# A narrower fifth turn in attention, with the last 64 keys' low parts made on VectorE

## The chip, the cores and the metric

The kernel runs on one core of one Trainium2 chip. The metric is the device time of one execution in microseconds (us); lower is better. TensorE (PE in the profile) multiplies matrices and writes to PSUM; its weight loads are shown as an engine of their own, PEld. VectorE is DVE, ScalarE is ACT, GpSimd is POOL, and SyncE (SP) issues the transfers.

## The reference

Three stages follow each other: attention with a threshold on four batches of 576 tokens and 8 heads of 64, a feed-forward layer with squared ReLU, and a mixture of eight experts of which each token takes one. The change is in the first stage alone. Cut to its core, that stage is:

```
scores = scale * np.matmul(q, k.transpose(0, 1, 3, 2))          # (4, 8, 576, 576)
thresh = np.max(scores, axis=-1, keepdims=True) - tau
scores = np.where(scores >= thresh, scores, -1000000000.0)
scores = scores - np.max(scores, axis=-1, keepdims=True)
attn = np.exp(scores)
attn = attn / (np.sum(attn, axis=-1, keepdims=True) + 1e-09)
attn_out = np.matmul(attn, v)
x = attn_out.transpose(0, 2, 1, 3).reshape(4 * 576, 512)
x = _moe_ref(x, w_in, w_out)      # np.maximum(x @ w_in, 0) ** 2 @ w_out
return _moe2_ref(x, w_gate, w_output_gate, w1, w2)              # top expert of eight
```

## The kernel before

**Precision.** Values that must be exact enough to choose an expert are split into a high part (rounded to the format float32r) and a low part (what is left), and a product is made of hi·hi, hi·lo and lo·hi.

**Pairs and chunks.** Attention runs over 16 pairs of heads (4 batches of 4 pairs; `pr` is the pair's number, `NP` is 4). A pair has 9 chunks of 128 query rows. A chunk goes through these steps, each on one engine:

1. scores (PE, L647): 128 x 576 into one of two PSUM buffers;
2. the row maximum (DVE, L650), the exponential (ACT, L653), the threshold (ACT, L658), mask and row sum (DVE, L662);
3. the reciprocal of the sum (POOL L667, DVE L670) and the normalisation of the 576 columns of the buffer `p` (POOL L673, or ACT L705);
4. outside the first batch, two small steps on POOL, `tail1` and `tail2` (L499 on 64 columns, and L718): they put the low parts of the last 64 keys into columns 576 to 639 of `p`, beside their plain values in columns 512 to 575;
5. the turn (PE, L727): five transposes of 128 x 128, one for each 128 columns of `p`, into one PSUM buffer of five blocks, `pT`. There is one `pT` buffer. The fifth block holds the last 64 keys in its rows 0 to 63, and in rows 64 to 127 their low parts (zeros in the first batch);
6. the evacuation of `pT`: in the first batch one copy on ACT (L738). Later ACT rounds all five blocks to the high part (`hi`, L744), and then DVE subtracts it from the first four blocks (`lo`, L747) to get the low part. When `lo` is done, `pT` is free for the next turn.

Then `t_av` multiplies the turned probabilities with the values: in plain float32 for the first batch (L788), in high and low parts after it (L770).

**What else runs in the stage.** The preparation of the next pair transposes k and q on PE (L570) and splits them on ACT (L578, L580) and DVE (L586, L588); its PSUM buffers are the two `pM` buffers, which `t_av` and the feed-forward matmuls (L866) use too. From the second batch on, feed-forward matmuls of finished batches are laid between the chunks. In the second batch DVE, ACT and POOL also convert the weights `w_in`.

**The order.** No order is written by hand. Every step is handed to a planner, `g.add(engine, duration, function, reads, writes, key)`. The planner lays the steps out with those assumed durations, takes the earliest that can start and among these the one with the smallest key, and hands out the buffers. The instructions then run on each engine in that order and wait for each other by semaphores. So a changed duration or a removed step moves others on all engines.

Of the kernel before, what the change touches and what calls it, by code (L numbers as in the profile page):

```python
# [257 lines left out]
def moa(ctx, tc, q, k, v, tau, w_in, w_out, wg, wog, w1, w2, ctab, coln, out):  # L258
    nc = tc.nc
    B, H, S, D = 4, 8, 576, 64  # L260
    P = 128
# [233 lines left out]
    for x in ALL["p"].slots:  # L495
        nc.gpsimd.memset(x.view[:, S:], 0.0)

    def gcopy(out, in_):
        nc.gpsimd.tensor_scalar(out, in_, 1.0, 1.0, op0=ALU.mult, op1=ALU.mult)  # L499

# [125 lines left out]
    def t_chunk(n, key):  # L626
# [79 lines left out]
                  key + K("norm", pr))  # L706
        else:
            g.add("POOL", 0.73, nrm, [sm], [p], key + K("norm", pr))
        if not full(pr, 0):
            ph = new("pk", n)  # L710
            last, low = slice(512, S), slice(S, NQ * P)

            def tail1():
                gcopy(ph.t, p.t[:, last])

            def tail2():

                nc.gpsimd.tensor_tensor(p.t[:, low], p.t[:, last], ph.t.bitcast(F32), op=ALU.subtract)  # L718

            g.add("POOL", 0.16, tail1, [p], [ph], key + K("norm", pr))  # L720
            g.add("POOL", 0.27, tail2, [ph], [p], key + K("norm", pr))
# [2 lines left out]

        def tr():
            for j in range(NQ):
                nc.tensor.transpose(ps.t[:, j], p.t[:, j * P : (j + 1) * P], ident)  # L727

        g.add("PE", 0.545, tr, [p], [ps], key + K("turn", pr))
        for j, gi, c0, w, off in PARTS[st]:  # L730
            h = 2 * pr + j
            whole = full(pr, j)
            if (h, gi) not in ptb:
                ptb[h, gi] = new("ptf" if whole else "pt", f"{h}_{gi}")
            pt = ptb[h, gi]
            if whole:
                g.add("ACT", c_act(NQ * w, True),
                      lambda pt=pt, c0=c0, w=w, off=off: nc.scalar.activation(  # L738
                          pt.t[:, :, off : off + w], ps.t[:, :, c0 : c0 + w], AF.Copy),
                      [ps], [(pt, 0, off)], key + K("parts", pr))  # L740
                continue

            def hi(pt=pt, c0=c0, w=w, off=off):
                nc.scalar.activation(pt.t[:, :NQ, off : off + w], ps.t[:, :, c0 : c0 + w], AF.Copy)  # L744

            def lo(pt=pt, c0=c0, w=w, off=off):
                nc.vector.tensor_tensor(  # L747
                    pt.t[:, NQ:, off : off + w], ps.t[:, : NQ - 1, c0 : c0 + w],
                    pt.t[:, : NQ - 1, off : off + w].bitcast(F32), op=ALU.subtract,
                )  # L750

            g.add("ACT", c_act(NQ * w, True), hi, [ps], [(pt, 0, off)], key + K("parts", pr))
            g.add("DVE", c_dve(4 * w), lo, [ps, (pt, 0, off)], [(pt, 1, off)], key + K("parts", pr))

    def t_av(pr, j, gi, key):
        h = 2 * pr + j
        pt = ptb.pop((h, gi))
        N = GN[gi]
        vb = vh.get(pr)
        ps = Buf(pM, f"av{h}_{gi}")  # L760
        if pr not in xfb:
            xfb[pr] = new("xf", pr)
        xf = xfb[pr]
        mine = slice(64 * j, 64 * j + 64)
        other = slice(64 - 64 * j, 128 - 64 * j)
        cols = slice(GOFF[gi], GOFF[gi] + N)

        def mm(lo):
            for c in range(NQ - 1, 2 * NQ - 1) if lo else range(NQ - 1):
                nc.tensor.matmul(  # L770
                    ps.t[:, :N], vb.t[:, j, c % NQ].rearrange("p a d -> p (a d)"), pt.t[:, c, :N],
                    start=(c == 0), stop=(c == 2 * NQ - 2),
                )

        def e1():
            nc.scalar.activation(xf.t[mine, cols], ps.t[other, :N], AF.Copy)

        def e2():
            nc.vector.tensor_tensor(xf.t[mine, cols], ps.t[mine, :N], xf.t[mine, cols], op=ALU.add)

        offs = [0, 128] if gi == 0 else [0, 128, 256]
        if full(pr, j):
            raw = raws[pr, "v"]

            def mm1():
                for c in range(NQ):
                    kr = QSZ[c]
                    nc.tensor.matmul(ps.t[:64, :N], raw.t[:kr, j, c], pt.t[:kr, c, :N],  # L788
                                     start=(c == 0), stop=(c == NQ - 1))

            g.add("PE", NQ * 4 * N * 0.4227e-3 + 0.06, mm1, [(pt, 0, o) for o in offs] + [(raw, j), (raw, 2)], [ps], key, hold=[xf])
            g.add("ACT", c_act(N, True), lambda: nc.scalar.activation(xf.t[mine, cols], ps.t[:64, :N], AF.Copy),
                  [ps], [(xf, j, gi)], key)
            return
        for hl in range(2):
            rd = [(pt, x, o) for o in offs for x in range(1 + hl)] + [(vb, j, x) for x in range(2)]
            g.add("PE", (NQ - 1 + hl) * c_pe(N), lambda hl=hl: mm(hl), rd, [ps], key, hold=[xf])
        g.add("ACT", c_act(N, True), e1, [ps], [(xf, j, gi)], key)
        g.add("DVE", c_dve(N), e2, [ps], [(xf, j, gi)], key)
# [629 lines left out]
```

## Time and profile before

| | |
|---|---|
| median of 3 runs | 1042.99 us (1042.43 to 1044.68) |
| profiled execution | 1044.39 us, of which the span of its instructions is 1042.6 us |
| granted TensorE clock over the span | 0.993 of full speed |
| PE busy | 95% of the span |
| PEld busy | 84% |
| DVE, ACT, POOL busy | 66%, 62%, 33% |

By the timestamps of the turn the four batches of attention take about 16 to 484 us: the first until about 124 us, the second until about 240 us, the third and fourth until about 484 us. Each batch has 36 chunks. A busy PE is not the same as a PE at its peak: matmuls overlap, and the record of one matmul (270 to 400 ns) is longer than the distance to the next one. The distance from start to start tells what a matmul costs in a row of them.

### The profile page before, as it was taken

What the parts mean: (1) busy time and instruction counts of PE and PEld (TensorE: products, weight loads), DVE (VectorE), ACT (ScalarE), POOL (GpSimd) and SP (SyncE); (2) the same over time, 40 slices, a digit from 0 to 9 for tenths busy, and PEclk for the clock granted to TensorE, in tenths of its full rate; (3) what the DMA queues carried; (4) which work ended last, traced back from release to release, by engine and by line L of the source; (5) the groups of instructions that cost most, each with busy time, mean ns of one, the idle gap of its engine ahead of it and who ended that gap; (6) DMA issues with size and microseconds to landing.
All of it is one profiled execution on the core that took longest, in us unless ns stands there. A gap on an engine that the chain in (4) does not pass through costs nothing.

```text
span 1042.6 us, 19065 instructions
## 1 busy us (share of the span) xinstructions
PE 995.4 (95%) x6276; PEld 876.4 (84%) x6276; DVE 693.0 (66%) x1563; ACT 645.3 (62%) x1347; POOL 345.2 (33%) x660
## 2 busy tenths in 40 slices
PE   6999888999999999999999999999999999999995
PEld 5666588889999999999998888888789988888884
DVE  4768989987877777885652444434587768767730
ACT  5778776676766666766643444444665668767730
POOL 1233788675665666562000000010112211211200
PEclk9999989999999999999999999999999999999998
DMA  6555766554455554544882344433757868877700
GB/s 150 123 135 143 174 169 173 159 135 126 119 124 142 141 136 122 154 121 130 248 254 60 104 120 118 118 108 82 222 166 262 289 204 283 292 256 256 277 21 24
DMA packets 165438, 167.86 MB, mean 161 GB/s; under 512 B 60367, under 2 KB 126159, under 8 KB 165330
## 3 DMA queue, kind: packets, MB, share of 16 engines
q1 hardware_dynamic: 161090, 156.03, 52.3%
q0 software_dynamic: 4096, 10.52, 3.1%
q8 instruction: 52, 0.85, 0.4%
q14 instruction: 56, 0.46, 0.2%
q10 hardware_dynamic: 144, 0.00, 0.0%
HBM read 110.72 MB, written 29.56 MB: 135 GB/s over the span
## 4 chain that ended last, share of the span: by engine, by line
PE 72%; DMA 8%; DVE 8%; issue 5%; ACT 4%; POOL 1%; SPq 0%; DVEq 0%; POOLq 0%; ACTq 0%
PE bank L981 17%; PE bank L866 14%; PE bank L1295 9%; PE bank L1245 8%; PE bank L727 6%; PE bank L647 6%; PE bank L770 5%; PE bank L788 3%; DMA memf<-in_moe_w_dram 2%; DMA memf<-in_moe_w_out_dram 2%; DVE memf L650 1%; DMA out_dram<-memf 1%; PE bank L1100 1%; PE bank L1265 1%; DVE memf L662 1%
## 5 line engine op out<-in xcount | busy, mean ns | idle before, releaser
L866 PE MATMUL bank<-memr,w 128*128 128x288 f32 x1536 | 228.9, 299 | 4.5 <-ACT memf L872 2.5
L866 PEld LDWEIGHTS bank<-memr,w 128*128 128x128 f32 x1536 | 209.8, 188 | 9.1 <-ACT memf L872 4.8
L981 PE MATMUL bank<-w,memr 128*128 128x512 f32 x648 | 157.4, 394 | 0.0
L981 PEld LDWEIGHTS bank<-w,memr 128*128 128x128 f32 x648 | 119.1, 188 | 23.4
L662 DVE SCALAR_TENSOR_TENSOR memf<-bank,memf 128x576 f32<-128x576 f32 x144 | 115.7, 813 | 34.5 <-ACT memf L653 33.6
L647 PE MATMUL bank<-memr 128*128 128x288 f32 x600 | 112.0, 315 | 7.1 <-DVE memf L662 6.7
L727 PE MATMUL bank<-ident,memf 128*128 128x128 f32 x720 | 106.4, 279 | 10.7 <-ACT ptf L738 5.0
L650 DVE TENSOR_REDUCE memf<-bank 128x1 f32<-128x576 f32 x144 | 106.2, 748 | 12.3 <-PE bank L647 9.5
L1086 POOL DMA_INDIRECT lst<-memf x18 | 18.1, 1008 | 267.5 <-DVE memf L1072 202.8
L673 POOL TENSOR_SCALAR memf<-memf 128x576 f32<-128x576 f32 x128 | 97.4, 765 | 26.4 <-DVE memf L670 14.5
L653 ACT ACTIVATE memf<-bank,memf 128x576 f32<-128x576 f32 x144 | 104.1, 734 | 0.2
L727 PEld LDWEIGHTS bank<-ident,memf 128*128 128x128 f32 x720 | 82.8, 142 | 23.3 <-issue 7.0
L647 PEld LDWEIGHTS bank<-memr 128*128 128x128 f32 x600 | 87.1, 194 | 12.1 <-DVE memf L662 10.0
L744 ACT ACTIVATE memr<-bank 128x640 fp32r<-128x640 f32 (+1 forms) x120 | 76.7, 650 | 22.8 <-PE bank L727 21.0
L1245 PE MATMUL bank<-memr,w 128*128 128x256 f32 x564 | 89.0, 283 | 0.6 <-DVE memr L1255 0.5
L966 DVE TENSOR_TENSOR memr<-memf,memr 128x512 fp32r<-128x512 f32 x72 | 48.3, 699 | 59.3 <-ACT memf L963 59.2
L1230 DVE TENSOR_TENSOR w<-memf,w 128x512 fp32r<-128x512 f32 x114 | 74.5, 687 | 13.6 <-ACT w L1227 10.8
L667 POOL TENSOR_SCALAR memf<-memf 128x1 f32<-128x1 f32 x144 | 31.3, 217 | 149.0 <-DVE memf L662 131.7
L747 DVE TENSOR_TENSOR memr<-bank,memr 128x512 fp32r<-128x512 f32 (+1 forms) x120 | 74.4, 628 | 8.3 <-ACT memr L744 7.2
L1245 PEld LDWEIGHTS bank<-memr,w 128*128 128x128 f32 x564 | 77.4, 191 | 1.8 <-DVE memr L1255 1.0
L1295 PE MATMUL bank<-memr 128*128 128x512 f32 x306 | 77.3, 393 | 0.0
L1230 DVE TENSOR_TENSOR memr<-memf,memr 128x512 fp32r<-128x512 f32 x94 | 62.7, 688 | 21.3 <-ACT memr L1227 14.8
(144 smaller groups left out, 1725.9 us busy)
## 6 DMA issues: line engine op xcount, KB each, us to landing
memf<-in_moe_w_dram SPq DMA_DIRECT2D x104, 512.0 KB
r_scr<-memf SPq DMA_DIRECT2D x128, 144.0 KB
memf<-r_scr SPq DMA_DIRECT2D x36, 512.0 KB
memr<-memr SPq DMA_DIRECT2D x64, 144.0 KB
memr<-memr SPq DMA_DIRECT2D x64, 128.0 KB
memr<-memr SPq DMA_DIRECT2D x32, 256.0 KB
memf<-in_moe_w_in_dram SPq DMA_DIRECT2D x16, 512.0 KB
memf<-in_moe_w_out_dram SPq DMA_DIRECT2D x16, 512.0 KB
```

The lines of the kernel that those rows point to most:

```text
L647: nc.tensor.matmul(s.t[:, hf, :HALF], qo, ko[:, halves[hf]], start=(i == 0), stop=(i == len(ops) - 1))
L650: nc.vector.tensor_reduce(nm.t, s.t[:, :, :HALF], axis=AX.XY, op=ALU.max, negate=True)
L653: nc.scalar.activation(p.t[:, :S].rearrange("p (a n) -> p a n", a=2), s.t[:, :, :HALF], AF.Exp, bias=nm.t)
L662: nc.vector.scalar_tensor_tensor(p3, s.t[:, :, :HALF], th.t, p3, op0=ALU.is_ge, op1=ALU.mult, accum_out=sm.t)
L673: nc.gpsimd.tensor_scalar(p.t[:, :S], p.t[:, :S], sm.t, 1.0, op0=ALU.mult, op1=ALU.mult)
L727: nc.tensor.transpose(ps.t[:, j], p.t[:, j * P : (j + 1) * P], ident)
L744: nc.scalar.activation(pt.t[:, :NQ, off : off + w], ps.t[:, :, c0 : c0 + w], AF.Copy)
L866: nc.tensor.matmul(ps.t[:, :HALF], wv[:, a, kc], xT.t[:, x, kc, half], start=(i == 0), stop=(i == len(seq) - 1),)
L981: nc.tensor.matmul(ps.t, s.t[:, fc], wob[fc].t[:, x], start=(fc == 0 and i == 0), stop=(fc == NFC - 1 and i == 2))
L1230: lambda i=i, w=w, raw=raw: nc.vector.tensor_tensor(w.t[:, 1], raw.t[:, i], w.t[:, 0].bitcast(F32), op=ALU.subtract),
L1245: nc.tensor.matmul(ps.t[:, :256], w1b[kc][fc // 4].t[:, a, (fc % 4) * P : (fc % 4 + 1) * P], x2.t[:, x, kc], start=(i == 0), stop=(i == 11))
L1295: nc.tensor.matmul(ps.t, hT.t[:, a, fc, u * P : (u + 1) * P], w2b[fc].t[:, x], start=(fc == 0 and i == 0), stop=(fc == 7 and i == 2))
```

## The change

The fifth turn transposes only the 64 columns of the last keys, so that it writes 64 rows of the fifth block, in every chunk of the first, third and fourth batch (108 of the 144 chunks). In the second batch (`early_low`) all stays as it was. For the third and fourth batch `tail1` and `tail2` on POOL are gone. In their place a new DVE step after `lo` subtracts the high part from rows 0 to 63 of the fifth block and writes the difference to rows 64 to 127 of the evacuated tile. Each chunk has one such step of 128 columns, the fifth of a pair's chunks has two of 64. The low-part matmuls of `t_av` wait for this step too. The planner's duration for a turn falls from 0.545 to 0.49 in the changed batches. One memset at the start clears the rows of `pT` that the narrow turn no longer writes.

```
+    nc.vector.memset(pT.slots[0].view()[64:, NQ - 1], 0.0)
...
-        if not full(pr, 0):
+        early_low = NP <= pr < 2 * NP
+        if early_low:
             ph = new("pk", n)
...
         def tr():
             for j in range(NQ):
-                nc.tensor.transpose(ps.t[:, j], p.t[:, j * P : (j + 1) * P], ident)
-
-        g.add("PE", 0.545, tr, [p], [ps], key + K("turn", pr))
+                m = P if j < NQ - 1 or early_low else 64
+                nc.tensor.transpose(ps.t[:m, j], p.t[:, j * P : j * P + m], ident)
+
+        g.add("PE", 0.545 if early_low else 0.49, tr, [p], [ps], key + K("turn", pr))
...
             g.add("DVE", c_dve(4 * w), lo, [ps, (pt, 0, off)], [(pt, 1, off)], key + K("parts", pr))
+            if not early_low:
+                g.add("DVE", 0.08 + w / 600,
+                      lambda pt=pt, c0=c0, w=w, off=off: nc.vector.tensor_tensor(
+                          pt.t[64:, NQ - 1, off : off + w], ps.t[:64, NQ - 1, c0 : c0 + w],
+                          pt.t[:64, NQ - 1, off : off + w].bitcast(F32), op=ALU.subtract),
+                      [ps, (pt, 0, off)], [(pt, 2, off)], key + K("parts", pr))
...
-            rd = [(pt, x, o) for o in offs for x in range(1 + hl)] + [(vb, j, x) for x in range(2)]
+            rd = [(pt, x, o) for o in offs for x in ((0, 1, 2) if hl else (0,))] + [(vb, j, x) for x in range(2)]
```

Two places show how the order moves. The first is on DVE, in the third batch, where a pair's q is prepared. `bank_2_73` is `pT`, `bank_1_68` and `bank_1_69` are the `pM` buffers, `bank_2_77` and `bank_2_78` are the score buffers. Before:

```order
L586 TENSOR_TENSOR memr<-bank_1_68,memr 128x384
L747 TENSOR_TENSOR memr<-bank_2_73,memr 128x4x128
L586 TENSOR_TENSOR memr<-bank_1_69,memr 128x192
L650 TENSOR_REDUCE memf<-bank_2_77 128x1
L588 SCALAR_TENSOR_TENSOR memr<-bank_1_68,qsc,memr 128x320
L650 TENSOR_REDUCE memf<-bank_2_78 128x1
L747 TENSOR_TENSOR memr<-bank_2_73,memr 128x4x128
L588 SCALAR_TENSOR_TENSOR memr<-bank_1_69,qsc,memr 128x256
```

And now, where the lines after the inserted code are up to 12 numbers higher (L747 is L753, the new step is L762):

```order
L589 TENSOR_TENSOR memr<-bank_1_69,memr 128x384
L673 RECIPROCAL memf<-memf 128x1
L753 TENSOR_TENSOR memr<-bank_2_73,memr 128x4x128
L762 TENSOR_TENSOR memr<-bank_2_73,memr 64x128
L589 TENSOR_TENSOR memr<-bank_1_68,memr 128x192
L591 SCALAR_TENSOR_TENSOR memr<-bank_1_69,qsc,memr 128x320
L653 TENSOR_REDUCE memf<-bank_2_77 128x1
L653 TENSOR_REDUCE memf<-bank_2_78 128x1
L591 SCALAR_TENSOR_TENSOR memr<-bank_1_68,qsc,memr 128x256
L753 TENSOR_TENSOR memr<-bank_2_73,memr 128x4x128
```

The new step stands right behind `lo`, and the first split of q (128x320) stands ahead of both row maxima, where it had one of them ahead of it.

The second place is on PE, in the third batch, towards the end of a pair's chunks. Before:

```order
L727 MATMUL bank_2_73<-ident,memf 128x128 x5
L866 MATMUL bank_1_69<-memr,w_84 128x288 x8
L647 MATMUL bank_2_78<-memr 128x288 x4
L866 MATMUL bank_1_68<-memr,w_84 128x288 x4
L727 MATMUL bank_2_73<-ident,memf 128x128 x5
L866 MATMUL bank_1_68<-memr,w_84 128x288 x8
L770 MATMUL bank_1_69<-memr 128x320 x9
L570 MATMUL bank_1_68<-ident,memf 128x128 x3
```

And now:

```order
L733 MATMUL bank_2_73<-ident,memf 128x128 x4
L733 MATMUL bank_2_73<-ident,memf 64x128
L878 MATMUL bank_1_68<-memr,w_88 128x288 x4
L650 MATMUL bank_2_77<-memr 128x288 x4
L878 MATMUL bank_1_69<-memr,w_88 128x288 x8
L733 MATMUL bank_2_73<-ident,memf 128x128 x4
L733 MATMUL bank_2_73<-ident,memf 64x128
L878 MATMUL bank_1_69<-memr,w_88 128x288 x4
L782 MATMUL bank_1_68<-memr 128x320 x9
L573 MATMUL bank_1_69<-ident,memf 128x128 x3
```

A turn still has five matmuls; the fifth writes 64 rows of 128 columns instead of 128 rows. Between two turns there still lie 12 feed-forward matmuls and four of a score, and in the last stretch of the pair four feed-forward matmuls where there were eight.

## Rows read from the trace of the kernel before

**Rows 1.** The page, busy time and share of each engine.

```profile
PE 995.4 (95%) x6276; PEld 876.4 (84%) x6276; DVE 693.0 (66%) x1563; ACT 645.3 (62%) x1347; POOL 345.2 (33%) x660
```

**Rows 2.** Busy time by stretch: first batch, second batch, third and fourth.

```profile
core 0: us, PE busy (x) PEld busy (x) DVE busy (x) ACT busy (x) POOL busy (x), PEclk, DMA share, GB/s
16.00:124.00 108.00, 98.28 (x543) 66.92 (x543) 79.82 (x186) 84.80 (x177) 39.89 (x76) 1.00 0.58 141
124.00:240.00 116.00, 105.98 (x755) 97.93 (x754) 103.07 (x222) 81.57 (x174) 91.29 (x169) 0.97 0.61 158
240.00:485.00 245.00, 243.56 (x1872) 237.88 (x1871) 194.08 (x443) 165.39 (x361) 144.58 (x336) 1.00 0.50 132
```

**Rows 3.** Waits of PE and PEld, 259 to 437 us: total, times, longest us.

```profile
PEld bank L866 <- DVE memr L588: 2.7, 6, 0.5
...
PE bank L866 <- DVE memr L588: 1.3, 6, 0.2
```

**Rows 4.** Lines by shape, 259 to 437 us: count, busy us, mean ns, idle before.

```profile
L727 PE MATMUL bank<-ident,memf 128*128 128x128 f32 x274 | 39.0, 273 | 0.0
...
L747 DVE TENSOR_TENSOR memr<-bank,memr 128x512 fp32r<-128x512 f32 x48 | 32.8, 682 | 1.8 <-ACT memr L744 1.6
...
L727 PEld LDWEIGHTS bank<-ident,memf 128*128 128x128 f32 x275 | 31.5, 140 | 0.8
...
L718 POOL TENSOR_TENSOR memf<-memf,memr 128x64 f32<-128x64 f32 x54 | 17.3, 324 | 3.5
...
L499 POOL TENSOR_SCALAR memr<-memf 128x64 fp32r<-128x64 f32 x54 | 13.0, 245 | 3.4
...
L747 DVE TENSOR_TENSOR memr<-bank,memr 128x256 fp32r<-128x256 f32 x12 | 4.5, 420 | 0.4
```

**Rows 5.** Timeline of turns and plain float32 matmuls: start us, length us, count.

```profile
330.77 0.71 PE L727 MATMUL bank<-ident,memf 128*128 128x128 f32 x5
...
330.72 0.20 PEld L727 LDWEIGHTS bank<-ident,memf 128*128 128x128 f32 x2
...
61.17 1.78 PE L788 MATMUL bank<-ptf,memf 128*64 128x320 f32 x6
```

**Rows 6.** Lines by shape, whole span: the plain float32 matmul.

```profile
L788 PE MATMUL bank<-ptf,memf 128*64 128x320 f32 x64 | 18.9, 439 | 0.0
```

**Rows 7.** Timeline of weight loads with fewer than 128 columns, and of those behind them.

```profile
60.58 0.19 PEld L788 LDWEIGHTS bank<-ptf,memf 128*64 128x64 f32 x2 [0.16 <-issue]
...
63.56 0.31 PEld L727 LDWEIGHTS bank<-ident,memf 128*128 128x128 f32 x3 [0.49 <-issue]
...
597.28 1.05 PEld L1015 LDWEIGHTS bank<-memr 128*32 128x32 f32 x8
...
598.34 0.31 PEld L981 LDWEIGHTS bank<-w,memr 128*128 128x128 f32 x2
```

**Rows 8.** Timeline of `lo` on DVE and of the turn's loads, third batch.

```profile
329.92 0.69 DVE L747 TENSOR_TENSOR memr<-bank,memr 128x512 fp32r<-128x512 f32 x1
...
333.07 0.69 DVE L747 TENSOR_TENSOR memr<-bank,memr 128x512 fp32r<-128x512 f32 x1
...
330.72 0.53 PEld L727 LDWEIGHTS bank<-ident,memf 128*128 128x128 f32 x5
...
333.87 0.53 PEld L727 LDWEIGHTS bank<-ident,memf 128*128 128x128 f32 x5
...
326.46 0.76 DVE L747 TENSOR_TENSOR memr<-bank,memr 128x256 fp32r<-128x256 f32 x2
```

**Rows 9.** Timeline around the split of q, third batch.

```profile
342.35 0.75 DVE L650 TENSOR_REDUCE memf<-bank 128x1 f32<-128x576 f32 x1
343.01 0.54 DVE L588 SCALAR_TENSOR_TENSOR memr<-bank,qsc,memr 128x320 fp32r<-128x320 f32 x1
...
342.14 0.53 ACT L580 ACTIVATE memr<-bank,qsc 128x320 fp32r<-128x320 f32 x1
...
343.60 3.28 PEld L866 LDWEIGHTS bank<-memr,w 128*128 128x128 f32 x24 [0.45 <-DVE memr L588]
```

## The prediction

> **What bounds the kernel now.** I read the busy time of the page first. PE is busy for 95% of the span [rows 1]; the reader is to see that no other engine comes near it. A mean over the whole span says little about a change to attention, so the stretches come next [rows 2]. They differ. In the third and fourth batch PE is busy for 243.56 of 245 us. In the first batch it is busy for 98.28 of 108 us, and in the second, which the change leaves alone but for the order, for 105.98 of 116 us, with DVE at 103.07. So in the third and fourth batch only two things can count: what shortens PE's own work, and what makes PE wait. The waits come third: in the 178 us from 259 to 437, six pairs of heads, PE and its weight loads have one wait worth naming, the feed-forward matmuls that wait for DVE to split q, 2.7 us for six pairs [rows 3]. No wait on POOL is among them. Last come the timelines, from which the spacing of matmuls and the distance from one step to the next are read [rows 5 to 9].
>
> **The narrow turn itself.** Five turns take 0.71 us from the first start to the last end, and one record is 0.273 us long [rows 4, 5]. So they follow each other by (0.71 - 0.273) / 4 = 0.109 us. Either the weight load sets this or the moving operand does. The load: two loads with records of 0.140 us take 0.20 us together, so the second starts 0.06 us after the first [rows 4, 5]; a load of 128 columns holds the next one up for 0.06 us, not for 0.109. The moving side: six plain float32 matmuls of 320 columns take 1.78 us with records of 0.439 us [rows 5, 6], which is (1.78 - 0.439) / 5 = 0.268 us each, or 0.84 ns a column; 128 columns at that rate are 0.107 us. That fits. In a transpose the 64 or 128 columns of `p` are the loaded operand and the 128 columns of the identity move; the order shows a fifth turn of 64 x 128, so the identity still moves all its 128 columns. I take a saving of nothing. The bounds: half a turn for each of 108 chunks, 108 x 0.055 = 5.9 us less, if the load did set the pace; and a loss, if a load of 64 columns empties the array first (the last rival).
>
> A rule of the Trainium skill stands against this reading: "TensorE: Matmul & The Clock Gate", section on LDWEIGHTS, has a load cost its columns divided by 1.2 GHz, 107 ns for 128 columns and 53 ns for 64. By that rule the turn would be bound by its load and the narrow one would give back 54 ns, an estimate of 5.8 us in all. The 0.06 us between two loads of turns disagrees with it, so I carry it as a rival only.
>
> **The two POOL steps that go.** They are 72 times 0.245 + 0.324 us [rows 4], 41 us of POOL, and 0.57 us of the way from the normalisation to the turn. PE waits for POOL nowhere in these batches [rows 3], and the turn has no idle time before it [rows 4]. What releases a turn is `pT`: its loads start at 330.72 and 333.87, 0.11 us behind the ends of `lo` at 330.61 and 333.76 [rows 8]. Earlier values in `p` don't help such a turn. I take nothing; the upper bound of a gain is nothing too as long as `pT` is what comes last.
>
> **The new DVE step.** No row shows it. `lo` takes 0.682 us on 512 columns and 0.420 on 256 [rows 4], so 1.02 ns a column, which gives 0.289 us for 128 columns and 0.224 for 64. Two steps of 0.42 us in a row take 0.76 [rows 8], so a step adds 0.08 us less than its record: 0.21 and 0.14 us. A pair has eight of the first and two of the second, 1.96 us; eight pairs make 15.7 us of DVE. Its load in the third and fourth batch rises from 194.1 to 209.8 of 245 us, 86%, below the 89% of the second batch [rows 2]. As a sum that is hidden beside PE. Not as a delay: `pT` is released 0.21 us later, and a turn that already stands right behind `lo` makes PE wait for it, with scores and feed-forward matmuls queued behind. The rows show two such turns in a pair of nine; with one more that has little left, the old order would lose 2 to 3 x 0.21 = 0.42 to 0.63 us a pair, 3.4 to 5.0 us in eight pairs. The planner knows the step, though, and with 0.293 us counts it dearer than the 0.21 it adds, so it lays the turns for it; the second place of the order shows as much PE work between two turns as before. I take 0.25 us a pair, near the middle of 0 and 0.63: +2.0 us; the ends are 0 and 5.0. That DVE steps behind it start later is in these ends.
>
> **What the new order moves.** The one wait of PE hangs on the split of q. In the pair shown, ACT has the high part ready at 342.67, but DVE is in a row maximum from 342.35 to 343.10 and begins the split at 343.01; the feed-forward loads then start at 343.60 after 0.45 us of waiting [rows 9]. Now the split stands ahead of that maximum. It could begin at about 342.72, 0.29 us earlier. Eight pairs: -2.3 us; the ends are 0 and 8 x 0.45 = -3.6 us. Two maxima come later by this, and the score buffers with them; that is in the delay above.
>
> In the first and second batch no step gets shorter or longer on the chip. The order differs, since the planner counts a turn 0.055 us too low. PE's idle time there is 108 - 98.28 + 116 - 105.98 = 19.7 us [rows 2]. An order can give or take some of it and I see no sign for either; I take 0, with ends of 3 us either way, about a seventh of that idle time. The memset is one DVE step, below the 0.42 us of the row with 256 columns, ahead of all attention: nothing, or at the worst that.
>
> **Sum.** 0 (turn) + 0 (POOL) + 2.0 (DVE step) - 2.3 (split of q) + 0 (first two batches) = -0.3 us. Against the profiled execution of 1044.39 us that gives 1044.1 us. It ran 1.4 us above the median of the runs, so the forecast for the median is 1042.99 - 0.3 = 1042.7 us. Its own range, with the ends of the terms, is 1040 to 1045.5. About 0.2% (2.1 us) is what a measurement of this kernel can tell from no change.
>
> **Rivals.**
>
> First, the load does set the pace of the turn and the narrow turn is 0.055 us shorter. In the third and fourth batch 72 x 0.055 = 3.9 us come off an engine that never stops; in the first, 36 x 0.055 = 2.0 us come off one that stands idle for 9%, so between none and all. With the rest of the sum that is 1037 to 1039, say 1038 us. For it speaks that spacing and half of it would fit; against it the 0.06 us between loads.
>
> Second, the order gains more than I count: the shorter way to the turn lets the planner draw scores and turns apart, and some 3 us of the 19.7 us of idle time in the first two batches, or of the waits on the split of q, close: 1039.5 us. For it: PE does stand idle there. Against it: nothing that those batches do is cheaper.
>
> Third, slower: `pT` becomes what paces the third and fourth batch. Three of nine turns a pair are late by the whole 0.21 us, 5.0 us in eight pairs, and the split of q gains nothing, since the row maxima put behind it delay the scores instead: 1048 us. It decides from the point at which a turn's loads start 0.11 us behind the new step in three turns of a pair or more. For it: PE has no slack there, and DVE, in whose queue `lo` and the new step stand behind masks and maxima, is busy for 79% of the stretch already [rows 2]. Against it: the planner counts the step too dear rather than too cheap.
>
> Fourth, much slower: a load of 64 columns empties the array. Such loads in the plain float32 matmuls begin after 0.16 us of idle time, and the turn behind them after 0.49, while loads of 32 columns in float32r come without any, on either side [rows 7]. Going in and out would cost between 0.2 and 0.5 us a chunk, 72 x 0.35 = 25 us in the third and fourth batch alone: 1068 us. The rows allow both, as they differ in kind of matmul too. The Trainium skill, "TensorEngine Tiling (Array Packing)", says under its key properties that a change of tiling mode drains the engine, and under its restrictions that column tiling and float32 transposes exclude each other; by the second the narrow turn would not change the mode, and the 32-column loads agree with that as far as they go.
>
> **How the numbers follow.** The forecast has 0.40, the first rival 0.10, the second 0.20, the third 0.26, the fourth 0.04. Of the forecast's share 0.32 lies within 0.2%, 0.04 on each side. The first rival gives 0.09 to faster and 0.01 to the same, the second 0.17 and 0.03; the third 0.22 to slower and 0.04 to the same; the fourth all to slower. Together: faster 0.30, same 0.40, slower 0.30. The range reaches to the first rival below, 1037, and a little past the third above, 1049.5; the fourth and the tails are left out.
>
> **What would show it.** Five turns of a chunk still 0.71 us from start to end, with 0.109 us from the fourth to the fifth and on to the next load: the first step is right; 0.05 us there would make it wrong. The new step at about 0.29 us, directly behind `lo`. PE busy for all but 2 us of the third and fourth batch, and a turn's loads at 0.11 us behind the new step in not more than two of nine turns; more of them, with waits of PE for that step, would be the third rival. The wait for the split of q down from 0.45 us to about 0.15. Idle time ahead of the fifth turn's load would be the fourth rival. Third and fourth batch within 2 us of 245; a difference in the first two batches larger than 3 us would make the forecast wrong without any of its steps.

## The result and the profile after

The changed kernel takes 1050.42 us (median of 9 runs, 1047.36 to 1056.61); the kernel before, on the same chip, 1044.59 us (9 runs, 1042.43 to 1046.70). The ratio is 1.0062, with a 95% interval of 1.0045 to 1.0078: slower by 0.6%, some 6 us. The forecast was no change, with a range up to 1049.5. The profiled execution took 1050.42 us with a span of 1048.6.

The page's busy times, against [rows 1]:

```profile
PE 999.9 (95%) x6276; PEld 874.2 (83%) x6276; DVE 713.1 (68%) x1644; ACT 646.8 (62%) x1347; POOL 306.0 (29%) x516
```

DVE has 81 more steps (80 of the new kind and the memset) and 20 us more, POOL 144 steps and 39 us less. By stretch, against [rows 2]:

```profile
16.00:124.00 108.00, 98.46 (x541) 65.89 (x541) 77.69 (x186) 85.50 (x178) 41.77 (x75) 1.00 0.57 141
124.00:240.00 116.00, 106.68 (x771) 98.58 (x770) 101.98 (x224) 81.92 (x176) 90.12 (x170) 0.99 0.62 161
240.00:485.00 245.00, 242.90 (x1827) 232.09 (x1826) 214.51 (x516) 163.40 (x354) 104.08 (x192) 1.00 0.48 125
```

In the second batch PE starts more matmuls than before (771 against 755), in the third and fourth fewer (1827 against 1872): the first half runs ahead, the second falls behind. A clearer measure is the pair of heads. Taking the start of each pair's first turn, the pairs of the third batch begin 1.9 us earlier than before (249.3 against 251.2 us). From there a pair takes 30.26 us instead of 29.53 (mean of five, from the start of the tenth pair to that of the fifteenth), and the last turn of attention comes 5.1 us late, at 487.7 against 482.6 us. The first loads of the tenth and the fifteenth pair, before:

```profile
280.68 0.58 PEld L727 LDWEIGHTS bank<-ident,memf 128*128 128x128 f32 x5
...
428.31 0.58 PEld L727 LDWEIGHTS bank<-ident,memf 128*128 128x128 f32 x5
```

And after:

```profile
279.43 0.50 PEld L733 LDWEIGHTS bank<-ident,memf 128*128 128x128 f32 x5 [0.17 <-issue]
...
430.71 0.50 PEld L733 LDWEIGHTS bank<-ident,memf 128*128 128x128 f32 x5 [0.17 <-issue]
```

This length of a pair is the measure in the experiments below, since it is free of what happens in the first half and behind attention. It is read from one trace of each version; a version below that leaves these batches as they were repeats it to 0.01 us.

The waits of PE and PEld in the same 178 us as [rows 3]:

```profile
PEld bank L733 <- issue: 3.4, 12, 0.4
PEld bank L573 <- DVE memr L589: 1.0, 6, 0.2
PEld bank L650 <- DVE memf L665: 1.0, 6, 0.2
PE bank L733 <- DVE memr L762: 1.2, 6, 0.2
```

The wait for the split of q is gone from the list. In its place PE waits for DVE at turns (L733), at the next pair's transposes of q and k (L573) and at scores (L650). "Issue" ahead of L733 names no engine, but the loads that stop there begin 0.12 us behind the end of the new step L762. (The transposes had a wait of 1.1 us before, too, put down to issue.) The operations, by shape, against [rows 4]:

```profile
L753 DVE TENSOR_TENSOR memr<-bank,memr 128x512 fp32r<-128x512 f32 x48 | 32.6, 679 | 1.9 <-ACT memr L750 1.7
L733 PEld LDWEIGHTS bank<-ident,memf 128*128 128x128 f32 x212 | 23.5, 140 | 4.9 <-issue 3.4
L733 PE MATMUL bank<-ident,memf 128*64 128x128 f32 x53 | 14.4, 273 | 0.0
L762 DVE TENSOR_TENSOR memr<-bank,memr 64x128 fp32r<-64x128 f32 x48 | 13.6, 284 | 1.4
L733 PEld LDWEIGHTS bank<-ident,memf 128*64 128x64 f32 x53 | 5.9, 111 | 0.0
L762 DVE TENSOR_TENSOR memr<-bank,memr 64x64 fp32r<-64x64 f32 x12 | 2.6, 218 | 0.2
```

The records are as forecast: 0.284 us for the new step, and a fifth turn of 0.273 us like the others, whose load has a shorter record (111 instead of 140 ns), with no idle time ahead. What was not forecast stands between the records. DVE around the new step, and the turn that waits for it (against [rows 8]):

```profile
350.29 0.69 DVE L753 TENSOR_TENSOR memr<-bank,memr 128x512 fp32r<-128x512 f32 x1
351.02 0.28 DVE L762 TENSOR_TENSOR memr<-bank,memr 64x128 fp32r<-64x128 f32 x1
351.33 0.82 DVE L665 SCALAR_TENSOR_TENSOR memf<-bank,memf 128x576 f32<-128x576 f32 x1
...
351.42 0.50 PEld L733 LDWEIGHTS bank<-ident,memf 128*128 128x128 f32 x5
```

`lo` ends at 350.98 and the new step starts at 351.02; it ends at 351.30 and the mask starts at 351.33. Most DVE steps in a row in the kernel before overlap by about 0.08 us, as two `lo` do in [rows 8]. Here nothing overlaps, on either side. Over the 64 steps of 128 columns the median gap (from the end of one record to the start of the next) is +31 ns ahead, and behind +31 to +33 ns, by neighbour. The 16 steps of 64 columns have +13 ns ahead and +13 to +31 ns behind.

### The profile page after: what moved, and what is told of

Same layout as the page of the kernel before. It is cut to its first block, busy times and chain, and to the rows that moved or that the text cites. A ratio compares the mean times of both kernels' runs of the same rounds, so it can differ in the third digit from the quotient of the medians.

```text
span 1048.6 us, 19022 instructions
## 1 busy us (share of the span) xinstructions
PE 999.9 (95%) x6276; PEld 874.2 (83%) x6276; DVE 713.1 (68%) x1644; ACT 646.8 (62%) x1347; POOL 306.0 (29%) x516
## 4 chain that ended last, share of the span: by engine, by line
PE 70%; DMA 10%; DVE 8%; issue 6%; ACT 4%; POOL 2%; SPq 1%; POOLq 0%; ACTq 0%; DVEq 0%
PE bank L993 17%; PE bank L878 13%; PE bank L1307 8%; PE bank L1257 7%; PE bank L733 6%; PE bank L650 6%; PE bank L782 4%; PE bank L800 4%; DMA out_dram<-memf 2%; DMA memf<-in_moe_w_dram 2%; DMA memf<-in_moe_w_in_dram 2%; DVE memr L753 2%; DVE memf L653 1%; DVE memf L665 1%; PE bank L573 1%
## 5 line engine op out<-in xcount | busy, mean ns | idle before, releaser
L665 DVE SCALAR_TENSOR_TENSOR memf<-bank,memf 128x576 f32<-128x576 f32 x144 | 115.6, 814 | 17.6 <-ACT memf L656 15.5
L733 PE MATMUL bank<-ident,memf 128*128 128x128 f32 (+1 forms) x720 | 107.0, 280 | 13.2 <-ACT ptf L744 4.3
L650 PE MATMUL bank<-memr 128*128 128x288 f32 x600 | 110.7, 313 | 7.2 <-DVE memf L665 7.0
L733 PEld LDWEIGHTS bank<-ident,memf 128*128 128x128 f32 (+1 forms) x720 | 77.5, 138 | 29.6 <-issue 13.1
L650 PEld LDWEIGHTS bank<-memr 128*128 128x128 f32 x600 | 86.1, 192 | 13.9 <-DVE memf L665 11.2
L753 DVE TENSOR_TENSOR memr<-bank,memr 128x512 fp32r<-128x512 f32 (+1 forms) x120 | 75.1, 628 | 10.0 <-ACT memr L750 9.3
```

What stands on the lines that cost most here:

```text
L650: nc.tensor.matmul(s.t[:, hf, :HALF], qo, ko[:, halves[hf]], start=(i == 0), stop=(i == len(ops) - 1))
L665: nc.vector.scalar_tensor_tensor(p3, s.t[:, :, :HALF], th.t, p3, op0=ALU.is_ge, op1=ALU.mult, accum_out=sm.t)
L733: nc.tensor.transpose(ps.t[:m, j], p.t[:, j * P : j * P + m], ident)
L753: nc.vector.tensor_tensor(pt.t[:, NQ:, off : off + w], ps.t[:, : NQ - 1, c0 : c0 + w], pt.t[:, : NQ - 1, off : off + w].bitcast(F32), op=A ...
```

## The experiments

"Pair" is the length of a pair of heads as above: 29.53 us before, 30.26 after. Times are medians, with the ratio to the kernel before on the same chip and its 95% interval; a version without a ratio was executed once.

**The step not issued.** The changed kernel's order, but DVE does not do the new step; the low parts of the last 64 keys are left out in the third and fourth batch.

```
-                      lambda ...: nc.vector.tensor_tensor(pt.t[64:, ...], ps.t[:64, ...], ...)
+                      lambda pt=pt: (None),
```

> The changed kernel with its order kept on every engine, but the new DVE step is not issued (so the low parts of the last 64 keys are left out in the third and fourth batch). Theory: the step is what costs, because it holds pT longer (in the changed kernel's trace it ends 0.31 us behind lo) and because DVE overlaps it with neither neighbour (0.43 us of DVE each). Without it a pair of the third and fourth batch falls from 30.3 back to 29.5 us or a little below, and the time to 1043 us (1041 to 1045), about 7 us below the changed kernel. Rival A, the order that the planner made (a turn counted at 0.49) is what costs: the time stays at 1049 to 1051. Rival B, the narrow turn costs: it stays there too.

1040.64 us, ratio 0.9974 (0.9957 to 0.9991), pair 29.25 us. PE and PEld keep one small wait in the 178 us:

```profile
PEld bank L573 <- issue: 1.2, 6, 0.2
```

The first loads of the tenth and the fifteenth pair:

```profile
277.60 0.55 PEld L733 LDWEIGHTS bank<-ident,memf 128*128 128x128 f32 x5
...
423.85 0.55 PEld L733 LDWEIGHTS bank<-ident,memf 128*128 128x128 f32 x5
```

So the whole loss hangs on the step: 30.26 - 29.25 = 1.01 us a pair. And the rest of the change gains 29.53 - 29.25 = 0.28 us a pair, the size of the split of q.

**The fifth turn wide again.**

```
-                m = P if j < NQ - 1 or early_low else 64
+                m = P
```

> The changed kernel with its order kept, but all five turns take 128 columns everywhere; the new DVE step overwrites what the wider turn adds. Theory: a turn is paced by the identity's 128 columns, so nothing changes: 1050 us within 1.5, five turns 0.71 us long, 0.109 us from turn to turn. Rival B, a load of 64 columns costs the array something on the way out: the time falls by 108 times up to 0.17 us where PE is the bound, to 1040 or so. If the narrow turn saved its half (0.055 us), the time would rise by 4 to 6 us, to 1055.

1048.89 us, ratio 1.0047 (1.0031 to 1.0062), pair 30.21 us: 0.05 us from the changed kernel. The fifth turn starts 0.109 us behind the fourth in both, as in the kernel before. The width of the turn does not count.

**Only the first batch changed.** The third and fourth keep `tail1` and `tail2` on POOL and the wide turn.

```
-        early_low = NP <= pr < 2 * NP
+        early_low = pr >= NP
```

> The change in the first batch alone: the narrow turn, counted at 0.49 by the planner; the third and fourth batch as the second, with the two POOL steps and no new DVE step. Theory: the third and fourth batch run as before, 29.5 us a pair. What is left is the order of the first and second batch, which stood 2 us ahead of the kernel before at the fifth to eighth pair of the changed kernel: if that is a property of the order, 1042.5 us (1041 to 1045), same or slightly faster than before. Rival A, the planner's lower cost of a turn makes a bad order: over 1047.

1041.74 us, ratio 0.9982 (0.9970 to 0.9994), pair 29.54 us. The third batch begins at 248.2 us, 3.0 us earlier than before, and the pairs are those of before, with the same wait for the split of q (2.7 and 1.3 us). By the total the order of the first two batches is worth 1.9 us (0.6 to 3.1).

**Dearer costs in the planner.** The step counted at 0.43 us, which is its record and the gaps, and the turn at 0.545 us.

```
-        g.add("PE", 0.545 if early_low else 0.49, tr, ...)
+        g.add("PE", 0.545, tr, ...)
-                g.add("DVE", 0.08 + w / 600,
+                g.add("DVE", 0.22 + w / 600,
```

> The changed kernel with truer costs in the planner: the new step at 0.22 + w/600 (0.433 us for 128 columns, what it takes from DVE), the turn at 0.545. Nothing else changes. Theory: the step's cost is real work on DVE and a real delay of pT, so a planner that knows it can only space the turns better: between 1045 and 1050 us, better than the changed kernel by 0 to 5, still not below the kernel before. Rival A, the planner's wrong costs are the whole loss: back at 1043 to 1045.

1053.81 us, ratio 1.0093 (1.0076 to 1.0110), against an expectation of 1045 to 1050 us. A pair takes 31.68 us in the profiled execution, which was the slowest of its seven (1058.96 us). The order now puts a turn at the seam of two pairs right behind its normalisation on POOL:

```profile
347.94 0.50 PEld L733 LDWEIGHTS bank<-ident,memf 128*128 128x128 f32 x5 [1.15 <-POOL memf L676]
```

In this case truer durations made a worse order.

**The same step, written to the rows it reads.** All operands in rows 0 to 63; this overwrites the high parts and leaves the low parts out. The wrong values change which tokens go to which expert, so only attention is compared.

```
-                          pt.t[64:, NQ - 1, off : off + w], ps.t[:64, NQ - 1, c0 : c0 + w],
+                          pt.t[:64, NQ - 1, off : off + w], ps.t[:64, NQ - 1, c0 : c0 + w],
```

> The changed kernel with its order kept; the new step writes its 64 rows to rows 0 to 63 instead of 64 to 127 (it overwrites high parts there and leaves the low parts out; only the time counts). In the changed kernel DVE starts the step 0.01 to 0.03 us after the end of the one before and the next one 0.03 us after its end, where other steps overlap by 0.08. Theory: this comes of the step's reading and writing different halves of the partitions. In the same rows the overlaps come back, the step adds 0.21 instead of 0.43 us of DVE and releases pT 0.1 us earlier, and a pair of the third and fourth batch takes 29.5 to 29.9 us instead of 30.25 (without the step 29.24). Rival: any step of 64 rows, or one that reads what the step before it worked on, starts so; then 30.2 as before.

Pair 29.32 us; the total, 1115.44 us, has other tokens in the experts and says nothing here. DVE around a step:

```profile
347.94 0.69 DVE L753 TENSOR_TENSOR memr<-bank,memr 128x512 fp32r<-128x512 f32 x1
348.55 0.27 DVE L762 TENSOR_TENSOR memr<-bank,memr 64x128 fp32r<-64x128 f32 x1
```

The step begins before `lo` ends, at 348.63. Its gaps are -82 ns ahead and -8 to -75 behind (medians by neighbour). The order of instructions is that of the changed kernel and DVE does as many elements; 0.94 of the 1.01 us are gone.

**`pT` not held by the step.** It takes both operands from the evacuated tile, so `pT` is free when `lo` ends; the low parts are left out (zeros).

```
-                          pt.t[64:, NQ - 1, off : off + w], ps.t[:64, NQ - 1, c0 : c0 + w],
+                          pt.t[64:, NQ - 1, off : off + w], pt.t[:64, NQ - 1, off : off + w].bitcast(F32),
```

> The changed kernel with its order kept; the new step reads both operands from the evacuated tile in SBUF and nothing from pT (so it writes zeros as low parts), and the next turn no longer waits for it. It still stands in DVE's queue with its full length. Theory 1, the hold of pT is what costs: a pair takes 29.3 to 29.6 us. Theory 2, the time on DVE is what costs, since lo of the next chunk stands behind it: a pair stays at 30.0 to 30.3 us. Without the step a pair takes 29.24.

1056.16 us, pair 30.37 us, with gaps of about +31 ns on both sides. The step itself became longer, 0.366 us in the mean instead of 0.284. That mean mixes two lengths, by what POOL does at the time:

```profile
342.98 0.75 POOL L676 TENSOR_SCALAR memf<-memf 128x576 f32<-128x576 f32 x1 [1.07 <-DVE memf L673]
...
343.43 0.43 DVE L762 TENSOR_TENSOR memr<-memr 64x128 fp32r<-64x128 f32 x1
...
347.06 0.28 DVE L762 TENSOR_TENSOR memr<-memr 64x128 fp32r<-64x128 f32 x1
```

In 29 of the 64 steps of 128 columns a POOL instruction that began earlier runs on for more than 0.2 us; they take 0.43 us (median) and end 0.135 us behind POOL's. The 27 that start with no POOL instruction under way take 0.285. In the changed kernel, where one operand comes from PSUM, there are as many of each kind, and they take 0.284 and 0.285 us. So this is not a clean test of the hold alone: `pT` was freed early and the pair became no shorter, but the steps took 0.8 us more of DVE a pair.

**The step issued twice.** The second one, which writes the same again, waits on a semaphore for the first.

> The changed kernel with its order kept, the new step issued twice in a row (the second writes the same values). The step costs 1.0 us a pair of the third and fourth batch (30.25 against 29.24 without it). Theory: pT is late by about 0.31 us more at each turn and PE has no room left, so a second one costs more than the first: a pair takes 31.7 to 32.5 us, ten steps of 0.2 or more each, and the time is 1062 us or more. Rival, the cost lies in something that happens once (the order, the first step's start): 30.3 to 30.8.

1068.94 us, pair 32.43 us: ten more steps a pair cost 2.17 us, more than the first ten. So the cost is not something that happens once. Most of the waiting stands at turns:

```profile
PEld bank L733 <- issue: 9.2, 17, 0.9
...
PE bank L733 <- DVE memr L762: 7.6, 21, 0.7
```

The second step takes DVE's time and holds `pT` too, so this run does not tell the two apart.

**The split of q first, without the step.** The version of "only the first batch", in which, from the second batch on, the maximum of a pair's fifth chunk waits for the first split of the next pair's q.

> The kernel with the narrow turn in the first batch alone (1041.74 us) and one thing more: in the third and fourth batch the row maximum of a pair's fifth chunk is made to come after the first split of the next pair's q on DVE, as it stands in the order of the changed kernel. Theory: the wait of PE for that split (0.45 us a pair) is shortened by 0.29 us, as in the run without the new step (29.24 against 29.53 us a pair): seven pairs, 2 us less, 1039.7 us (1038.5 to 1041.5), below both kernels. Rival, the 0.29 us there came of the missing POOL steps: no gain, 1041.7 or, since the planner moves other things too, more.

1043.10 us, ratio 0.9993 (0.9978 to 1.0008), pair 29.42 us. Of the 0.29 us a pair 0.12 came (29.54 to 29.42), and no gain in the total can be told. In the 178 us the wait for the split has fallen to 0.2 us, but there is a new one at turns, put down to the exponential:

```profile
PEld bank L734 <- ACT memf L656: 2.2, 6, 0.4
```

It stands ahead of the turn of each pair's sixth chunk, 0.36 us a time. That the maxima put behind the split make that chunk late is likely, but not shown. The planner's order, in which the split stands ahead of both maxima, has no such wait in the version without the step.

**The same values in both halves.** If crossing the halves costs the overlap, it can be avoided: POOL copies the 64 normalised columns beside themselves, the fifth turn is wide, and its rows 0 to 63 and 64 to 127 are the same. The step then writes the low parts into rows 0 to 63, and the high parts stay in rows 64 to 127. The buffer of `v` has the rows of the last 64 keys in both halves, so the products are the same. The planner counts turn and step as 0.545 and 0.213 us.

```
+        if pr >= 2 * NP:
+            g.add("POOL", 0.16, lambda: gcopy(p.t[:, S : NQ * P], p.t[:, 512:S]), [p], [p], ...)
...
-                g.add("DVE", 0.08 + w / 600,
+                g.add("DVE", w / 600,
...
-                          pt.t[64:, NQ - 1, off : off + w], ps.t[:64, NQ - 1, c0 : c0 + w],
+                          pt.t[:64, NQ - 1, off : off + w], ps.t[:64, NQ - 1, c0 : c0 + w],
```

> In the third and fourth batch GpSimd copies the last 64 columns of the normalised values beside themselves (one step of 64 columns a chunk), the fifth turn is 128 wide again, and so its rows 0 to 63 and 64 to 127 hold the same values. The new VectorE step now reads and writes rows 0 to 63 (the low parts land there, the high parts stay in 64 to 127). The planner counts the turn 0.545 us and the step 0.213 us. Theory (the cost of the step is that it does not overlap its neighbours when it goes from one half of the partitions to the other): the gaps ahead of and behind the step are again about -0.08 us, a pair of heads takes 29.4 to 29.6 us (30.26 in the changed kernel, 29.53 in the kernel before), the time is 1041 to 1043 us. Rival (any further VectorE step behind the subtraction costs this, wherever it writes): gaps +0.01 to +0.03 us, a pair 30.0 us or more, 1046 to 1050 us. Second rival (the GpSimd copy ahead of the turn is what the saved steps hid): waits of the turn's loads for GpSimd, a pair 29.8 or more.

1046.81 us, ratio 1.0029 (1.0014 to 1.0044), pair 30.00 us. The overlap is back (gaps of -83 ns ahead, -11 to -74 behind), yet the pair was missed: in this order one row maximum stands ahead of the split of q, as in the kernel before, and the wait for it is longer by the step:

```profile
PEld bank L881 <- DVE memr L591: 4.1, 6, 0.7
```

**The same with the changed kernel's planner durations**, so that PE's order in attention is that of the changed kernel and the split of q stands ahead of both maxima.

```
-                g.add("DVE", w / 600,
+                g.add("DVE", 0.08 + w / 600,
-        g.add("PE", 0.545 if pr >= NP else 0.49, tr, ...)
+        g.add("PE", 0.545 if early_low else 0.49, tr, ...)
```

> As the run with the copied rows, but with the planner's durations of the changed kernel (turn 0.49, step 0.293 us in the third and fourth batch), so that TensorE's order in attention is that of the changed kernel, with the split of q ahead of both row maxima. Theory (lost overlap is the whole loss, and that order is worth 0.29 us a pair): a pair takes 29.3 to 29.4 us and the time is 1040 to 1042 us, below the kernel before and beside the version that makes low parts on VectorE nowhere in the third and fourth batch. Rival (the step costs in itself, or the GpSimd copy does): a pair 29.9 us or more, 1045 us or more.

1041.17 us, ratio 0.9973 (0.9959 to 0.9987), pair 29.34 us: as expected, and faster than both kernels. It leaves nothing of the computation out. Most of the gain on the kernel before may come from the order of the first two batches: the version with only the first batch changed, whose pairs are those of before, has 0.9982, and the two intervals overlap. The third and fourth batch account for 0.19 us a pair, 1.5 us in eight pairs. DVE around the step (start, length):

```profile
346.24 0.69 DVE L756 TENSOR_TENSOR memr<-bank,memr 128x512 fp32r<-128x512 f32 x1
346.84 0.27 DVE L765 TENSOR_TENSOR memr<-bank,memr 64x128 fp32r<-64x128 f32 x1
```

The third and fourth batch by stretch, as in [rows 2]:

```profile
240.00:485.00 245.00, 245.00 (x1887) 240.15 (x1886) 204.60 (x521) 167.82 (x363) 121.47 (x265) 1.00 0.51 133
```

And the one wait of PE and PEld in the 178 us:

```profile
PEld bank L573 <- issue: 1.1, 6, 0.2
```

The step begins 0.09 us ahead of `lo`'s end at 346.93. DVE's busy time, 204.60 us, lies 13.5 us above that of the run without the step (191.09); in the changed kernel it is 23.4 above.

**The step wholly in rows 64 to 127**, with the planner durations of the first copied version. The low parts land in the upper rows.

```
+                          pt.t[64:, NQ - 1, off : off + w], ps.t[64:, NQ - 1, c0 : c0 + w],
+                          pt.t[64:, NQ - 1, off : off + w].bitcast(F32), op=ALU.subtract),
```

> As the run with the copied rows and its planner's durations, but the VectorE step reads and writes rows 64 to 127. If going from one half of the partitions to the other is what costs the overlap: gaps of about -0.08 us on both sides, a pair 29.4 to 29.6 us, as with rows 0 to 63. If it is the upper rows as such, as output or as input: gaps of +0.01 to +0.03 us, a pair about 30.2 us.

1056.44 us, pair 31.10 us, against 30.00 in rows 0 to 63, with gaps of +14 to +32 ns. Crossing from half to half within the step is not what costs; that theory of mine fell. Nor is it the upper rows as such. Once in this trace the step is followed by an instruction that also reads and writes rows 64 to 127 alone, an addition of the second head (L794), and these two overlap by 0.08 us:

```profile
495.02 0.29 DVE L765 TENSOR_TENSOR memr<-bank,memr 64x128 fp32r<-64x128 f32 x1
495.24 0.49 DVE L794 TENSOR_TENSOR memf<-bank,memf 64x320 f32<-64x320 f32 x1
```

**From the upper rows to the lower.** The very order, instruction by instruction on every engine, of the version with 29.34 us; only the rows of the step's inputs differ.

```
+                          pt.t[:64, NQ - 1, off : off + w], ps.t[64:, NQ - 1, c0 : c0 + w],
+                          pt.t[64:, NQ - 1, off : off + w].bitcast(F32), op=ALU.subtract),
```

> As the run with the copied rows and the changed kernel's planner durations, but the VectorE step reads rows 64 to 127 and writes rows 0 to 63: it goes from one half of the partitions to the other, and touches the upper half only as input. The run with the step wholly in rows 64 to 127 has shown that crossing is not needed for the gaps. If what counts is that the output lies in the upper rows: gaps of about -0.08 us on both sides and a pair of 29.3 to 29.4 us, as with the step in rows 0 to 63. If any operand in rows 64 to 127, or in both halves, is enough: gaps of +0.01 to +0.03 us and a pair of about 30.2 us.

1051.07 us, pair 30.41 us, 1.07 us more than its twin. DVE around a step (start, length):

```profile
344.93 0.69 DVE L756 TENSOR_TENSOR memr<-bank,memr 128x512 fp32r<-128x512 f32 x1
345.64 0.29 DVE L765 TENSOR_TENSOR memr<-bank,memr 64x128 fp32r<-64x128 f32 x1
345.97 0.82 DVE L665 SCALAR_TENSOR_TENSOR memf<-bank,memf 128x576 f32<-128x576 f32 x1
```

Its waits of PE and PEld in the 178 us:

```profile
PEld bank L736 <- POOL memf L502: 2.4, 6, 0.4
PEld bank L650 <- DVE memf L665: 1.5, 6, 0.3
PEld bank L736 <- issue: 1.1, 6, 0.2
PEld bank L573 <- DVE memr L589: 1.0, 6, 0.2
PE bank L736 <- DVE memr L765: 1.2, 6, 0.2
```

The gaps are back at +0.03 us and so are the changed kernel's waits, at the same places and of much the same sizes (2.4 and 1.1 us where it has 3.4 at the turns, 1.5 where it has 1.0 at scores). The wait put down to POOL's copy (L502) is one of them: its twin has the same copy and waits for it nowhere. So among steps that start at row 0 the output alone in the upper rows is enough (the changed kernel), and so are the inputs alone.

## Why the prediction was wrong

**The step that failed is the new DVE step, in its size.** The prediction let it overlap its neighbours, "so a step adds 0.08 us less than its record: 0.21 and 0.14 us", and took 0.25 us a pair, with 0.63 at most. It was measured at 1.01 us a pair (30.26 against 29.25 without the step), 8.1 us in eight pairs where +2.0 was reckoned. Three pairs of runs that differ in the rows alone show that the lost overlap is nearly all of it: 30.26 against 29.32, 30.41 against 29.34, 31.10 against 30.00, between 0.94 and 1.10 us each. With the overlap the step costs 0.07 to 0.09 us a pair in this order (29.32 and 29.34 against 29.25), inside the ends of the prediction.

How 1 us comes out of gaps: ahead of the step the gap goes from -83 to +31 ns, 0.11 us; behind it by 0.04 us where the mask follows (36 of the 80 steps) and by 0.06 to 0.11 elsewhere. Ten steps a pair then take some 1.8 us more of DVE than with the overlap. (The records add a little: 0.284 us, or 0.293 in the runs with upper inputs, against 0.272 in rows 0 to 63.) About half of that reaches PE: `pT` comes free some 0.11 us later, and the mask, the splits and the next `lo` in DVE's queue later still, until turns, scores and transposes wait for them.

The overlap was taken from `lo` behind `lo` [rows 8], both of which use all 128 rows. The trace of before held a nearer row, which the prediction did not use. L779 adds 64 rows of a head to the result: rows 0 to 63 for one head of a pair, rows 64 to 127 for the other (`mine`). DVE in the kernel before:

```profile
334.48 0.08 DVE L662 DVE_READ_ACCUMULATOR memf<-bank,memf 128x1 f32 x1
334.48 0.48 DVE L779 TENSOR_TENSOR memf<-bank,memf 64x320 f32<-64x320 f32 x1
334.89 0.74 DVE L650 TENSOR_REDUCE memf<-bank 128x1 f32<-128x576 f32 x1
...
340.06 0.16 DVE L670 RECIPROCAL memf<-memf 128x1 f32<-128x1 f32 x1 [0.50 <-POOL memf L667]
340.25 0.49 DVE L779 TENSOR_TENSOR memf<-bank,memf 64x320 f32<-64x320 f32 x1
340.77 0.56 DVE L586 TENSOR_TENSOR memr<-bank,memr 128x384 fp32r<-128x384 f32 x1
```

The same instruction overlaps on both sides for the first head (it ends at 334.96, the next starts at 334.89) and on neither for the second (0.03 us ahead and behind). With that row as the model the step costs its record of 0.28 us, 0.03 us ahead and behind, and the 0.08 us by which the next step no longer overlaps `lo`: 0.42 us, twice the 0.21 (in front of the mask, which overlaps by 0.01 us only, it is 0.36).

The Trainium skill states this, as a model: "VectorE: DVE Perf Modes", section "Two Vector instructions with no wait between them". An instruction starts only when all earlier VectorE instructions have finished if one of its inputs, or its output, starts in another group of 32 partitions than the last one that was read from, or written to, that memory. All five arrangements agree with it: rows 0 to 63 throughout keep the overlap, and an upper output, upper inputs or both lose it (gaps of +13 to +33 ns), on the step and on the one behind, which goes back to row 0. The one that does not go back, L794 at 495.24 above, overlaps, which agrees too. The page gives no price for it.

**What held.** The narrow turn is worth nothing, by the turn made wide again (0.05 us a pair) and by the fifth matmul's unchanged record and distance; neither the load's pace (the first rival) nor an emptied array (the fourth) shows. The split of q and POOL's two steps together were put at 0.29 us a pair, and the run without the step gains 0.28. Most of it is the split's by the idle time ahead of loads in the 178 us: from 2.9 to 1.5 us at feed-forward matmuls, from 0.8 to 0.0 at turns. That it is all the split's is not shown: with the POOL steps kept and the split moved by hand only 0.12 came, and a new wait of 0.36 us a pair stood at a turn. The first two batches were put at 0 with ends of 3 us: the changed kernel starts its third batch 1.9 us earlier, other versions with the same order there 1.3 to 3.2 us, which is the second rival's gain. What in that order saves it is open. It hides part of the loss: without it the forecast would have been further off.

**The third rival named the outcome, not all of its causes.** It had 1048 us at 0.26, from the point where a turn's loads start 0.11 us behind the new step in three turns of a pair; in the pair from 340.0 us on it is five of nine. But it had 0.21 us a step and no gain from the split of q; the gain did come, and the delay was 1 us a pair, not 0.63. That `pT` is held longer is part of the way from DVE to PE, by the waits at turns. The idle time ahead of PE's loads in the 178 us, in the changed kernel and without the step, is 4.9 and 0.0 us at turns, 1.7 and 0.6 at scores, 2.4 and 1.6 at transposes, 1.0 and 1.5 at feed-forward matmuls: 6.3 us more in six pairs. That is 1.05 us a pair, the whole loss. The line for turns without the step, beside the 4.9 above:

```profile
L733 PEld LDWEIGHTS bank<-ident,memf 128*128 128x128 f32 x275 | 30.8, 135 | 0.0
```

So some four fifths of it stand at turns. The waits at scores, for the mask (L665), and at transposes, for the split of k (L589), are not for `pT`: there DVE itself is late. At a turn the two can't be told apart, since a late `lo` and a late step both hold `pT`; how the microsecond divides between them stays open.

In sum, for the third and fourth batch: by the turns' starts seven pairs lose 5.6 us and the last one 1.4, and the first two batches had brought 1.9. That makes the 5.1 us at the last turn. The remaining 0.9 us, of the 6.0 by which the span grew, come behind attention and are not explained.

## What to carry to other kernels

Before an added step is priced by its neighbours' overlap, compare the partitions it reads and writes with theirs: in these traces a VectorE step on rows 64 to 127 among steps that start at row 0 costs its own length and the overlap on both sides. Here, writing a copy so that the step stays in rows 0 to 63 turned 0.6% slower into 0.3% faster, of which the order of the first two batches may be the larger part. And an order that a planner finds is part of the price: the same step cost 0.09 us a pair in one order, and in another the pair was 0.66 us longer.

## What was not expected of the hardware

A VectorE subtraction of 64 x 128 values with both operands in SBUF took 0.285 us where no GpSimd instruction was under way at its start. Where one on SBUF ran on for more than 0.2 us it took 0.43 us and ended 0.135 us behind it, as if it had waited for its end (29 steps of the run with `pT` not held). With one operand in PSUM it took 0.284 us in both cases. A mean over both kinds, 0.366 us, would have been taken for a price of SBUF operands. The load of 64 columns in a transpose has a record of 111 ns against 140, and the turn is no shorter for it.
